# Copying the last two row swaps of each batch on VectorE instead of sending them by DMA

## The chip, the cores and the metric

The kernel runs on one core of one Trainium2 chip. The time is the device time of one execution in microseconds, the median of a few executions. A change counts as faster or slower from 2% on. Three terms come up throughout: PSUM is where this kernel's matmuls write, in banks; an eviction copies a finished bank to SBUF, and the next matmul into that bank may have to wait for it; the granted clock is the share of TensorE's full clock that the profile shows for a stretch.

## The reference, cut to what matters

```python
def _attn_ref(x, w_r, w_i, b_r, b_i):          # x: (8, 3008, 256)
    X = np.fft.rfft(x, axis=1)
    Yr = Xr @ w_r - Xi @ w_i + b_r
    Yi = Xr @ w_i + Xi @ w_r + b_i
    # soft threshold with lam = 0.01 on Yr and Yi
    y = np.fft.irfft(Y, n=x.shape[1], axis=1)

def _moe_ref(x, w_in, w_out, s, b):            # x: (24064, 256), d_ff = 2048
    r = np.maximum(x @ w_in, 0.0)
    return (s * (r * r) + b) @ w_out
```

Everything becomes matmuls: the Fourier transforms of length 3008 = 94 x 32 are two small DFTs each, and the second half is a large two-layer product. The kernel spreads the DFT work of batch b over the large product of earlier batches, so that TensorE never runs dry.

## The kernel before

Only the middle stage of the DFT work matters here. For each batch from 1 to 7 it handles 12 units. A unit is transformed (`fwd_unit`), mixed with the weights and thresholded (`mix_unit`), and transformed back (`inv_unit`). Between the last two, the halves of the partitions and the real and imaginary parts have to change places: that is the row swap, four pieces of 64 partitions x 256 elements a unit.

```python
    hpool = ...(tc.tile_pool(name="psh", bufs=2, space=PSUM))
    fpool = ...(tc.tile_pool(name="psf", bufs=2, space=PSUM))     # one_bank() takes from here
    # ...
    def evac(dst, src, cols, scale=None):          # PSUM to SBUF on the engine with less planned work
        ta, td = 0.17 + cols / 1200.0, 0.15 + cols / 960.0
        if load["act"] + ta <= load["dve"] + td:
            load["act"] += ta
            ...                                    # ScalarE
        load["dve"] += td
        ...                                        # VectorE
    # ...
        def mix_unit(i):
            ps = one_bank().rearrange("p (r e) -> p r e", r=2)
            # ... 4 matmuls ...
            t, m = ring[0][:, i % 4], ring[0][:, 4 + i % 2]
            nc.vector.tensor_tensor(out=t, in0=ps, in1=..., op=ALU.add)       # L563, frees ps
            nc.vector.tensor_tensor(out=m, in0=t, in1=low, op=ALU.max)        # L568
            nc.vector.tensor_tensor(out=m, in0=m, in1=high, op=ALU.min)       # L569
            nc.vector.tensor_tensor(out=t, in0=t, in1=m, op=ALU.subtract)     # L570
            load["dve"] += 1.75
            z = ring[0][:, 6 + i % 6]
            for j in range(2):
                for r in range(2):
                    nc.sync.dma_start(                                        # L576, the swap
                        out=z[64 * r : 64 * r + 64, j], in_=t[64 * j : 64 * j + 64, r]
                    )
            zt[i] = z

        def inv_unit(i):
            ps = one_bank().rearrange("p (j e) -> p j e", j=2)
            z = zt.pop(i)
            for j in range(2):
                nc.tensor.matmul(ps[:, j, :], T_t[:, 2 * i + j, :], z[:, j, :], ...)   # L585
            # ...
            evac(v[:, h : h + 2, :], ps, 512)
            # ... every second unit: v to DRAM; after the last: load it back, turned (vs) ...

        for h in range(H // 2 + 3):                # H = 12
            for i in range(2):
                put(fwd_unit, 2 * h + i, H)
                put(mix_unit, 2 * h - 2 + i, H)
                put(inv_unit, 2 * h - 6 + i, H)    # two to three turns behind its mix
            put(sum_unit, h, H // 2)
            if h == H // 2:
                units += [lambda: None] * 2        # empty steps, to give the last swaps time
```

Units 0 to 9 have further mixes and transforms between their swap and their inverse DFT. Units 10 and 11 are the last, so nothing but the two empty steps and units 8 and 9 stands between.

Of the kernel before, what the change touches and what calls it, by code (L numbers as in the profile page):

```python
# [94 lines left out]
def kernel(  # L95
# [13 lines left out]
    nc = tc.nc  # L109
# [6 lines left out]
    H = NPAIR // 2  # L116
# [34 lines left out]
    load = {"act": 0.0, "dve": 0.0}  # L151

    def evac(dst, src, cols, scale=None):
# [3 lines that stand above are left out]
            if scale is None:  # L157
                return None, nc.scalar.copy(out=dst, in_=src)  # L158
            return None, nc.scalar.mul(out=dst, in_=src, mul=scale)
        load["dve"] += td  # L160
        if scale is None:
            return nc.vector.tensor_copy(out=dst, in_=src), None
        return nc.vector.tensor_scalar_mul(out=dst, in0=src, scalar1=scale), None
# [4 lines left out]
    def one_bank():  # L168
        return fpool.tile([P, 512], F32, name="psf", tag="psf")
# [342 lines left out]
    def s23_units(b):  # L512

        vd = dpool.tile([NPAIR, P, D], F16, name="vd", tag="vd")
        if not ring:
            ring.append(bigpool.tile([P, 12, 2, D], F16, name="ring", tag="corr"))
        xf = {}
        zt = {}
        hold = {}

        def fwd_unit(i):

            bank = one_bank()
            ps = bank.rearrange("p (r c j k) -> p r c j k", r=2, c=DC, j=2)
            t = us[(b, i // 3)]
            for j in range(2):
                q = (2 * i + j) % 6
                for dc in range(DC):
                    nc.tensor.matmul(  # L529
                        ps[:, :, dc, j, :], t[:, q, dc * P : (dc + 1) * P],  # L530
                        F_t[:, 2 * i + j, :], start=True, stop=True,
                    )
            xt = xfpool.tile([P, 3, DC, P], F16, name="xf", tag="xf")
            evac(xt[:, 1:3].rearrange("p r c k -> p (r c k)"), bank, 512)
            nc.vector.tensor_tensor(out=xt[:, 0], in0=xt[:, 1], in1=xt[:, 2], op=ALU.add)
            load["dve"] += 0.25
            xf[i] = xt

        def sum_unit(h):

            ps = one_bank().rearrange("p (i e) -> p i e", i=2)
            for i in range(2):
                for dc in range(DC):
                    nc.tensor.matmul(  # L544
                        ps[:, i, :], xf[2 * h + i][:, 0, dc], W_t[:, dc, 0],
                        start=(dc == 0), stop=(dc == DC - 1),
                    )
            s = mpool.tile([P, 2, D], F32, name="s", tag="m")
            nc.scalar.copy(out=s, in_=ps)
            load["act"] += 0.6  # L550
            hold[h] = s

        def mix_unit(i):
            ps = one_bank().rearrange("p (r e) -> p r e", r=2)
            xt = xf.pop(i)
            for r in range(2):
                for dc in range(DC):
                    nc.tensor.matmul(  # L558
                        ps[:, r, :], xt[:, 2 - r, dc], W_g[:, dc, r],
                        start=(dc == 0), stop=(dc == DC - 1),  # L560
                    )
            t, m = ring[0][:, i % 4], ring[0][:, 4 + i % 2]
            nc.vector.tensor_tensor(  # L563
                out=t, in0=ps, in1=hold[i // 2][:, i % 2].unsqueeze(1).to_broadcast([P, 2, D]),
                op=ALU.add,
# [7 lines that stand above are left out]
            z = ring[0][:, 6 + i % 6]  # L573
            for j in range(2):
                for r in range(2):
                    nc.sync.dma_start(  # L576
                        out=z[64 * r : 64 * r + 64, j], in_=t[64 * j : 64 * j + 64, r]
                    )
            zt[i] = z

        def inv_unit(i):
# [3 lines that stand above are left out]
                nc.tensor.matmul(  # L585
                    ps[:, j, :], T_t[:, 2 * i + j, :], z[:, j, :], start=True, stop=True
                )
            if i % 2 == 0:
                hold["v"] = vpool.tile([P, 4, D], F16, name="v", tag="v")
            v = hold["v"]  # L590
            h = 2 * (i % 2)
            evac(v[:, h : h + 2, :], ps, 512)
            if i % 2 == 1:
                nc.sync.dma_start(
                    out=vd[2 * i - 2 : 2 * i + 2].rearrange("q p e -> p q e"), in_=v
                )
            if i == H - 1:
                vv = vd.rearrange("q (k n) e -> (q k) (n e)", n=N2)
                for h in range(2):
                    t = vspool.tile([96, HW, D], F16, name="vs", tag="vs")  # L600
                    nc.sync.dma_start(
                        out=t.rearrange("k n e -> k (n e)"),
                        in_=vv[:, h * HW * D : (h + 1) * HW * D],
                    )
                    vs[(b, h)] = t

        units = []

        def put(f, i, n):
            if 0 <= i < n:  # L610
                units.append(lambda: f(i))

        for h in range(H // 2 + 3):
# [3 lines that stand above are left out]
                put(inv_unit, 2 * h - 6 + i, H)  # L617
            put(sum_unit, h, H // 2)
            if h == H // 2:
                units += [lambda: None] * 2  # L620
        return units
# [226 lines left out]
```

## Time and profile before

| | before |
|---|---|
| time, median (range) of 3 | 873.04 us (873.01 to 874.69) |
| span of the profiled run | 871.1 us |
| TensorE / VectorE / ScalarE busy | 96% / 80% / 74% |
| mean granted clock of TensorE | 0.994 |
| swaps by DMA | 336 of 32 KB |

TensorE bounds the kernel, so the table's other rows count only where they make it wait. The prediction shows the lines.

### The profile page before, as it was taken

Reading aid. Unit: us, or ns where it says so; the run is one execution under the profiler, and the core shown is the slowest. Engines: PE = TensorE matmul, PEld = TensorE weight load, DVE = VectorE, ACT = ScalarE, POOL = GpSimd, SP = SyncE. Lnnn points to the kernel's source line nnn. Section 1 sums busy time; section 2 is a strip of 40 time slices with the busy share of each in tenths; the row PEclk is TensorE's granted clock in tenths of the full one; section 3 lists DMA queues with packets and bytes.
Section 4 is the critical chain, followed back from the end, with each engine's and each line's share of the span. In section 5 each row is a group of like instructions: output and inputs, shape, how many; then the busy total and the mean of one; then the engine's idle time right before and its main releaser. Section 6 shows DMA issues by size and latency. Waiting matters only on the chain.

```text
span 871.1 us, 16955 instructions
## 1 busy us (share of the span) xinstructions
PE 838.8 (96%) x6580; PEld 599.4 (69%) x6580; DVE 693.4 (80%) x971; ACT 640.7 (74%) x848; POOL 32.8 (4%) x53
## 2 busy tenths in 40 slices
PE   4889999999899999999999999999999999999996
PEld 3757766777567766777667776777667777766665
DVE  6788977888778987888878988798877887776664
ACT  4687876787677886787777787787877778666662
POOL 4100000000000000000000000000000000000000
PEclk9999999999999999999999999999999999999999
DMA  8754366423664248522764236633364133411111
GB/s 187 130 120 119 90 156 160 140 57 81 163 147 133 79 107 226 135 65 74 175 165 121 68 94 168 168 92 85 86 189 120 50 86 103 116 31 38 37 39 53
DMA packets 109346, 96.90 MB, mean 111 GB/s; under 512 B 10318, under 2 KB 101714, under 8 KB 107922
## 3 DMA queue, kind: packets, MB, share of 16 engines
q1 hardware_dynamic: 103266, 81.41, 32.6%
q0 software_dynamic: 6000, 14.42, 10.2%
q8 instruction: 51, 0.84, 0.4%
q14 instruction: 29, 0.24, 0.1%
HBM read 52.54 MB, written 46.66 MB: 114 GB/s over the span
## 4 chain that ended last, share of the span: by engine, by line
PE 89%; DMA 5%; ACT 2%; DVE 2%; issue 1%; SPq 1%; POOL 0%; DVEq 0%; POOLq 0%
PE psh L689 36%; PE psa L758 36%; PE psf L558 4%; DMA ring<-ring 3%; PE psf L493 3%; PE psf L529 2%; PE psf L544 2%; PE psf L638 2%; PE psf L585 2%; DMA x<-in_x_dram 1%; ACT rt L696 1%; DVE T_t L291 1%; PE psh L357 1%; ACT yt L158 0%; ACT m L393 0%
## 5 line engine op out<-in xcount | busy, mean ns | idle before, releaser
L696 ACT ACTIVATE rt<-psh 128x1024 f32<-128x1024 f32 (+2 forms) x384 | 386.8, 1008 | 121.3 <-PE psh L689 119.6
L703 DVE TENSOR_TENSOR gt<-rt 128x1024 f16<-128x1024 f32 (+2 forms) x322 | 385.8, 1200 | 111.2 <-ACT rt L696 110.7
L758 PE MATMUL psa<-w_out_t,gt 128*128 128x256 f16 (+1 forms) x3024 | 455.5, 273 | 0.1
L758 PEld LDWEIGHTS <-gt 128*128 128x128 f16 (+1 forms) x3024 | 301.7, 101 | 188.3 <-issue 3.6
L689 PE MATMUL psh<-yt,w_in 128*128 128x512 f16 (+1 forms) x1344 | 398.5, 379 | 0.0
L689 PEld LDWEIGHTS <-w_in 128*128 128x128 f16 x1536 | 143.2, 98 | 26.0 <-issue 1.1
L768 DVE SCALAR_TENSOR_TENSOR ost<-psa,s_bc,bias_bc 128x512 f32<-128x512 f32 (+1 forms) x96 | 70.8, 737 | 8.9 <-PE psa L758 6.1
L158 ACT CAST v<-psf 128x512 f16<-128x512 f32 x79 | 46.0, 582 | 29.0 <-PE psf L585 28.4
L700 ACT ACTIVATE gt<-rt 128x1024 f16<-128x1024 f32 (+2 forms) x62 | 65.4, 1055 | 0.9
L563 DVE TENSOR_TENSOR ring<-psf,s 128x512 f16<-128x512 f32 x84 | 57.4, 683 | 3.4 <-PE psf L558 3.3
L158 ACT CAST u<-psf 96x512 f16<-96x512 f32 x79 | 45.7, 580 | 16.5 <-PE psf L493 16.2
L158 ACT CAST xf<-psf 128x512 f16<-128x512 f32 x78 | 45.7, 585 | 10.4 <-PE psf L529 10.4
L689 PE MATMUL psh<-tail,w_in 128*128 128x512 f16 (+1 forms) x192 | 52.1, 353 | 0.0
L558 PE MATMUL psf<-W_g,xf 128*128 128x256 f16 x336 | 50.4, 273 | 0.0
L158 ACT CAST yt<-psf 128x480 f16<-128x480 f32 (+2 forms) x71 | 36.4, 526 | 10.8 <-PE psf L638 10.7
L493 PE MATMUL psf<-x,A_t 94*96 94x512 f16 x104 | 39.9, 384 | 1.1 <-ACT yt L158 0.5
L585 PE MATMUL psf<-ring,T_t 128*128 128x256 f16 x168 | 33.2, 275 | 7.7 <-DMA ring<-ring 7.6
L569 DVE TENSOR_TENSOR ring<-ring,high 128x512 f16<-128x512 f16 x84 | 35.5, 422 | 2.1
L570 DVE TENSOR_TENSOR ring<-ring 128x512 f16<-128x512 f16 x84 | 35.4, 422 | 2.0
L568 DVE TENSOR_TENSOR ring<-ring,low 128x512 f16<-128x512 f16 x84 | 35.3, 420 | 1.5
L558 PEld LDWEIGHTS <-xf 128*128 128x128 f16 x336 | 32.9, 98 | 3.7
L182 POOL DMA_DIRECT2D x<-in_x_dram x32 | 16.7, 525 | 492.3 <-PE psf L493 456.0
(77 smaller groups left out, 479.3 us busy)
## 6 DMA issues: line engine op xcount, KB each, us to landing
out_dram<-ost SPq DMA_DIRECT2D x152, 128.0 KB
x<-in_x_dram POOLq DMA_DIRECT2D x32, 376.0 KB, 6.4
ud<-u SPq DMA_DIRECT2D x28, 384.0 KB
us<-ud SPq DMA_DIRECT2D x28, 384.0 KB
ring<-ring SPq DMA_DIRECT2D x336, 32.0 KB
vd<-v SPq DMA_DIRECT2D x42, 256.0 KB
vs<-vd SPq DMA_DIRECT2D x14, 768.0 KB
out_dram<-ost SPq DMA_DIRECT2D x16, 120.0 KB
```

The costliest lines, as they stand in the source:

```text
L158: return None, nc.scalar.copy(out=dst, in_=src)
L493: nc.tensor.matmul(ps[0:96, :], A_t[0:N1, :], x16[(b, c)][0:N1, j * D : (j + 2) * D], start=True, stop=True,)
L558: nc.tensor.matmul(ps[:, r, :], xt[:, 2 - r, dc], W_g[:, dc, r], start=(dc == 0), stop=(dc == DC - 1),)
L563: nc.vector.tensor_tensor(out=t, in0=ps, in1=hold[i // 2][:, i % 2].unsqueeze(1).to_broadcast([P, 2, D]), op=ALU.add,)
L569: nc.vector.tensor_tensor(out=m, in0=m, in1=high, op=ALU.min)
L585: nc.tensor.matmul(ps[:, j, :], T_t[:, 2 * i + j, :], z[:, j, :], start=True, stop=True)
L689: nc.tensor.matmul(o, w_in_t[dc][:, mc * P : (mc + 1) * P], r, start=(dc == 0), stop=(dc == DC - 1),)
L696: nc.scalar.activation(out=rt[:, :, 0:w], in_=ps[:, :, 0:w], func=AF.Relu)
L700: nc.scalar.activation(out=gt[:, :, 0:w], in_=rt[:, :, 0:w], func=AF.Square)
L703: nc.vector.tensor_tensor(out=gt[:, :, 0:w], in0=rt[:, :, 0:w], in1=rt[:, :, 0:w], op=ALU.mult)
L758: nc.tensor.matmul(ps[0:size, h, :], gts[(ti, mc // 2)][:, mc % 2, sub * size : (sub + 1) * size], w_out_t[:, mc, :], start=(mc == 0), sto ...
L768: nc.vector.scalar_tensor_tensor(out=ost[0:size, 0:k], in0=ps[0:size, 0:k], scalar=s_bc[0:size], in1=bias_bc[0:size, 0:k], op0=ALU.mult, o ...
```

## The change

The last two units of a batch have the least time for their swap. The change lets VectorE, which has just computed the data, copy the four pieces itself, without a queue and a landing. The balance of the evictions is told of 0.13 us a copy.

```diff
             z = ring[0][:, 6 + i % 6]
             for j in range(2):
                 for r in range(2):
-                    nc.sync.dma_start(
-                        out=z[64 * r : 64 * r + 64, j], in_=t[64 * j : 64 * j + 64, r]
-                    )
+                    o, a = z[64 * r : 64 * r + 64, j], t[64 * j : 64 * j + 64, r]
+                    if i < H - 2:
+                        nc.sync.dma_start(out=o, in_=a)
+                    else:
+                        nc.vector.tensor_copy(out=o, in_=a)
+                        load["dve"] += 0.13
             zt[i] = z
```

## The prediction

The forecast's sum is 873.0 - 7.6 (waits) - 1.0 (hidden in the records) - 3.4 (slow pace) + 0.5 (allowance for late PSUM banks) = 861.5 us. An estimate from the trace: the 64x384 copies in the row of L285 took 261 ns, and if the 64x256 ones take no longer, four need at most 1.04 us, eight 2.1 us and all 56 some 14.6 us, less than the 17 us that the prediction holds against them; with the 1.22 and 0.75 us in between, four still land 1.9 us before a matmul that comes after 4.9 us. "Enough" is said there of waits after which the clock fell.

> **What bounds the kernel now.** I read the page first, then the list of who waited for whom on TensorE, then the order of time around the longest waits, and last the busy time and granted clock of a few stretches.
>
> From the page:
>
> ```profile
> span 871.1 us, 16955 instructions
> ...
> PE 838.8 (96%) x6580; PEld 599.4 (69%) x6580; DVE 693.4 (80%) x971; ACT 640.7 (74%) x848; POOL 32.8 (4%) x53
> ...
> PE 89%; DMA 5%; ACT 2%; DVE 2%; issue 1%; SPq 1%; POOL 0%; DVEq 0%; POOLq 0%
> ```
>
> TensorE is busy 96% of the span and carries 89% of the chain that ended last. VectorE at 80% and ScalarE at 74% have some room. A change can only pay by removing time in which TensorE stands still or runs slowly. So the waits of TensorE come next (what waited, for what: us in total, times, longest):
>
> ```profile
> PE psh L320 <- DMA x<-in_x_dram: 9.9, 4, 6.2
> PE psf L585 <- DMA ring<-ring: 7.6, 6, 3.2
> PE psf L388 <- DVE g L367: 2.2, 1, 2.2
> ```
>
> The first and third belong to the start (the first batch, before 60 us), which the change does not touch. The second is the change's target: the inverse-DFT matmul waits six times for a row swap by DMA. All smaller entries are 1.1 us or less in total. So 7.6 us is what the list offers; the order of time shows what it leaves out. TensorE at the end of the second batch that has swaps:
>
> ```profile
> 231.62 0.38 PE L585 MATMUL psf<-ring,T_t 128*128 128x256 f16 x2
> ...
> 232.27 0.60 PE L758 MATMUL psa<-w_out_t,gt 128*128 128x256 f16 x4
> 236.05 0.63 PE L585 MATMUL psf<-ring,T_t 128*128 128x256 f16 x2 [3.18 <-DMA ring<-ring]
> 236.48 1.06 PE L689 MATMUL psh<-yt,w_in 128*128 128x512 f16 x2
> 237.33 1.06 PE L758 MATMUL psa<-w_out_t,gt 128*128 128x256 f16 x4
> ```
>
> Counting L585 pairs from the batch's start, 231.62 is unit 10 and 236.05 is unit 11, the last one. After the wait the same four matmuls of L758 take 1.06 us where they took 0.60 before: TensorE has become slow. The stretches (us, busy time of each engine, then PEclk, DMA share, GB/s) say why:
>
> ```profile
> 124.00:126.40 2.40, 0.37 (x4) 0.09 (x2) 1.92 (x3) 0.94 (x2) 0.00 (x0) 1.00 0.85 188
> 126.50:131.00 4.50, 4.50 (x20) 2.57 (x21) 1.05 (x2) 2.19 (x3) 0.00 (x0) 0.62 0.77 210
> ...
> 236.10:240.00 3.90, 3.89 (x15) 1.92 (x16) 0.69 (x1) 0.88 (x2) 0.00 (x0) 0.56 0.45 139
> 240.00:250.00 10.00, 10.00 (x70) 6.59 (x68) 6.78 (x6) 7.05 (x9) 0.51 (x1) 1.00 0.82 199
> ```
>
> The granted clock falls to 0.62 and 0.56 for about 4 us after each of the two longest waits, and TensorE counts as fully busy there, so neither the busy share nor the list of waits shows that loss. The six waits, read from the order of time, are 2.06 (first batch with swaps), 3.18 (second), 1.21 (third), 0.30 (fourth), 0.48 and 0.36 (fifth); the sixth and seventh have none. Every one of them stands before unit 10 or 11 of its batch, which are exactly the two that the change moves.
>
> Why those swaps are late, from the queue of SyncE (start us, us):
>
> ```profile
> 227.62 3.34 SPq L576 DMA_DIRECT2D ring<-ring  x4
> 231.05 0.53 SPq L500 DMA_DIRECT2D ud<-u  x1
> ```
>
> The four issues of unit 11 take from 227.62 to 230.96, and the matmul is released at 236.05, 5.1 us later, for 128 KB. The DMA share is 0.86 in that stretch[...].
>
> [...]here waits of 2.06 and 3.18 us were enough, and 1.21 us was not. [...] The trace has a close relative (mean ns after the bar's first number):
>
> ```profile
> L570 DVE TENSOR_TENSOR ring<-ring 128x512 f16<-128x512 f16 x84 | 35.4, 422 | 2.0
> ...
> L285 DVE COPY F<-F_c 64x384 f16<-64x384 f16 x4 | 1.0, 261 | 0.0
> ```
>
> [...]no instruction of the kernel before moves between halves, so the trace doesn't say whether that costs extra. [...]
>
> **The change part by part.** Removed: for units 10 and 11 of 7 batches, 4 transfers each, so 56 of the 336 swaps, and 56 issues of a median 587 ns, 33 us of SyncE's queue, which sets nothing by itself. Removed with them: all six waits. Their sum is 2.06 + 3.18 + 1.21 + 0.30 + 0.48 + 0.36 = 7.6 us. A gap is counted from the modelled end of a 273 ns record, while such matmuls start 0.11 us apart at full pace, so each gap hides another 0.16 us or so: 6 x 0.16 = 1.0 us. The slow stretches cost (1 - 0.62) x 4.5 + (1 - 0.56) x 3.9 = 1.7 + 1.7 = 3.4 us. Sum on the path: 7.6 + 1.0 + 3.4 = 12.0 us.
>
> Added: 56 VectorE copies of 64x256. [...] This lies beside TensorE. The copies follow the last subtraction of a unit, and its matmul comes late. In the batch with the least room (the seventh):
>
> ```profile
> 732.19 0.43 DVE L570 TENSOR_TENSOR ring<-ring 128x512 f16<-128x512 f16 x1
> ...
> 737.64 0.38 PE L585 MATMUL psf<-ring,T_t 128*128 128x256 f16 x2
> ```
>
> 5.0 us lie between the end of unit 11's subtraction and its matmul, and 4.9 us (119.16 to 124.10) for unit 10 of the first such batch. [...]even with a square (1.22 us) and an output eviction (0.75 us) put in between they land 2 us early.
>
> Moved: the balance of evictions is told of 8 x 0.13 = 1.04 us more VectorE work a batch, so about one eviction or square a batch goes to ScalarE, at most some 7 us on an engine with 26% room. The order within VectorE may shift a little, so some PSUM banks come free later. I allow 0.5 us for that. Result: 873.0 - 12.0 + 0.5 = 861.5 us.
>
> **The rivals.** First, VectorE becomes the bound at the end of a batch. For it: it is busy 9.27 of 11.0 us from 112 to 123 us[...]. Against it: 15 buffers for the squares lie between it and TensorE's second product, and the slack above. If PSUM banks came late by a microsecond in each batch, the time would be about 867 us. [...]
>
> Second, the wait moves to another transfer: to units 8 and 9, still by DMA, or to the load of the turned batch. For it: unit 9 of the first batch with swaps has its last issue end at 118.25 and its matmul at 123.01, 4.8 us, no more than the late swaps took. Against it: these come before the removed waits, never waited before, and have fewer transfers behind them. Only the first half rate removed brings later work nearer, by 1.7 us. This would give back 2 to 4 us: 864 to 866.
>
> Third, the gain is returned because VectorE and ScalarE use the waits to catch up (VectorE idled 4 us at 238 us). Against it: the sixth and seventh batches run the same program without a wait, and TensorE is busy 10.00 of 10.00 us from 728 to 738 at clock 1.00. If it held, the time would stay at 868 to 872.
>
> **Range and chances.** The floor is the whole 12.0 us and perhaps another 1 or 2 from stores and evictions that no longer queue behind swaps: 859. The ceiling for the range takes the second rival: 866. Faster by over 2% needs 855.6 us, 17.5 us less; TensorE has not that much to win outside the start: 3%. Slower by over 2% needs over 17 us of new waits, more than all the added VectorE work on the path: 2%. Within 2%: 95%.
>
> **What would show it right or wrong.** Right: 280 swaps by DMA and 56 copies[...]; no wait of L585 on swaps; the clock at 1.00 from 60 us on; TensorE busy some 838 us less the 3.4 us of slow pace. [...] A wait of L585 on VectorE, or of ScalarE's and TensorE's PSUM users on it near 120 or 230 us, would show the first rival; waits on units 8 and 9, or at L638, the second; no waits but a time above 868, the third. A changed order on TensorE itself would upset the whole sum.

## The result, and the profile after

The changed kernel took 863.37 us (median of 4, 861.07 to 863.97) against 873.02 us for the kernel before. The ratio is 0.988, with a 95% interval of 0.9859 to 0.9902: within 2%, but clear of noise. Ratios here and below are the mean time of one kernel's runs over that of the other's of the same rounds, so not quite the ratio of the medians.

The page of the changed kernel, the same three lines as were shown of before:

```profile
span 859.3 us, 16905 instructions
...
PE 833.5 (97%) x6580; PEld 598.2 (70%) x6580; DVE 700.1 (81%) x1019; ACT 643.2 (75%) x856; POOL 33.1 (4%) x53
...
PE 89%; DVE 4%; ACT 3%; DMA 2%; issue 1%; SPq 0%; POOL 0%; DVEq 0%; POOLq 0%
```

The span is 11.8 us shorter. DMA falls from 5% to 2% of the chain that ended last. TensorE is busy 5.3 us less although it runs the same 6580 matmuls: slow matmuls count as longer busy time (in the kernel before, four matmuls of L758 took 1.06 us after the longest wait and 0.60 us ahead of it). VectorE is busy only 6.7 us more, not 12.4, because the balance moved eight instructions from it to ScalarE.

What TensorE waited for from 64 us on, that is without the start (us in total, times, longest):

```profile
PE psf L493 <- ACT yt L158: 0.5, 3, 0.2
PE psf L493 <- DVE v L162: 0.5, 1, 0.5
```

The 7.6 us for swaps are gone, at units 8 and 9 too; one wait for VectorE's eviction of an inverse DFT is new. TensorE at the end of the second batch with swaps, where it had stood still for 3.18 us and then run slowly:

```profile
227.66 0.38 PE L588 MATMUL psf<-ring,T_t 128*128 128x256 f16 x2
228.31 0.60 PE L761 MATMUL psa<-w_out_t,gt 128*128 128x256 f16 x4
228.75 0.38 PE L588 MATMUL psf<-ring,T_t 128*128 128x256 f16 x2
229.40 0.60 PE L761 MATMUL psa<-w_out_t,gt 128*128 128x256 f16 x4
```

(The changed kernel's L588 and L761 are L585 and L758 of before.) Units 10 and 11 follow each other without a wait, and four matmuls keep their 0.60 us. The stretches with the former drops of the clock (the second one has moved ahead to 228), same columns as in the prediction (start and end; length; busy time of TensorE, its weight loads, VectorE, ScalarE and GpSimd with instruction counts; clock; DMA share; GB/s):

```profile
124.00:126.40 2.40, 2.40 (x19) 1.63 (x18) 2.40 (x3) 2.40 (x5) 0.00 (x0) 1.00 0.89 203
126.50:131.00 4.50, 4.50 (x32) 2.93 (x30) 3.16 (x4) 2.91 (x4) 0.00 (x0) 1.00 0.70 203
228.00:232.00 4.00, 4.00 (x29) 2.65 (x27) 3.02 (x4) 3.02 (x4) 0.00 (x0) 1.00 0.78 238
```

From 124.0 to 126.4 TensorE now does 19 matmuls instead of 4, and the clock stays at 1.00. The DMA engines are as busy as before there. The swaps that remain and the copies (duration in ns min/median/max, first and last start):

```profile
L578 SPq DMA_DIRECT2D ring<-ring x280: 461/587/1985, 82.4 to 713.7; - x140
...
L580 DVE COPY ring<-ring x56: 208/222/261, 119.6 to 722.5; 64x256 f16<-64x256 f16 x56
```

To compare runs, one more reading is useful. The first matmul of the output bias (L296) starts at 63.4 us before and at 63.5 us after; all of the change lies behind it. From there to the end it is 807.7 us before and 795.8 us after. That 11.9 us is the whole gain. I call these two parts the start and the rest.

### The profile page after: what moved, and what is told of

Read it like the earlier page. It is cut to its first block, busy times and chain, and to the rows that moved or that the text cites. A ratio compares the mean times of both kernels' runs of the same rounds, so it can differ in the third digit from the quotient of the medians. Undisturbed runs are those within 1.5% of the kernel's fastest.

```text
span 859.3 us, 16905 instructions
## 1 busy us (share of the span) xinstructions
PE 833.5 (97%) x6580; PEld 598.2 (70%) x6580; DVE 700.1 (81%) x1019; ACT 643.2 (75%) x856; POOL 33.1 (4%) x53
## 4 chain that ended last, share of the span: by engine, by line
PE 89%; DVE 4%; ACT 3%; DMA 2%; issue 1%; SPq 0%; POOL 0%; DVEq 0%; POOLq 0%
PE psh L692 36%; PE psa L761 36%; PE psf L558 4%; PE psf L493 3%; PE psf L529 2%; PE psf L544 2%; PE psf L588 2%; PE psf L641 2%; DMA x<-in_x_dram 1%; DVE gt L706 1%; ACT rt L699 1%; DVE T_t L291 1%; ACT yt L158 1%; PE psh L357 0%; ACT m L393 0%
## 5 line engine op out<-in xcount | busy, mean ns | idle before, releaser
L761 PE MATMUL psa<-w_out_t,gt 128*128 128x256 f16 (+1 forms) x3024 | 453.9, 272 | 0.1
L761 PEld LDWEIGHTS <-gt 128*128 128x128 f16 (+1 forms) x3024 | 301.0, 101 | 186.9 <-issue 1.7
L563 DVE TENSOR_TENSOR ring<-psf,s 128x512 f16<-128x512 f32 x84 | 57.4, 683 | 3.5 <-PE psf L558 3.4
L158 ACT CAST xf<-psf 128x512 f16<-128x512 f32 x82 | 48.0, 585 | 11.1 <-PE psf L529 11.1
L158 ACT CAST u<-psf 96x512 f16<-96x512 f32 x78 | 45.1, 580 | 12.3 <-PE psf L493 12.1
L158 ACT CAST yt<-psf 128x480 f16<-128x480 f32 (+2 forms) x76 | 38.5, 518 | 14.4 <-PE psf L641 14.4
L641 PE MATMUL psf<-C_t,vs 96*128 96x96 f16 x448 | 32.9, 205 | 0.0
```

What stands on the lines that cost most here:

```text
L158: return None, nc.scalar.copy(out=dst, in_=src)
L563: nc.vector.tensor_tensor(out=t, in0=ps, in1=hold[i // 2][:, i % 2].unsqueeze(1).to_broadcast([P, 2, D]), op=ALU.add,)
L641: nc.tensor.matmul(ps[:, j * 96 : (j + 1) * 96], vs[(b, h)][:, k, ec * P : (ec + 1) * P], C_t, start=True, stop=True,)
L761: nc.tensor.matmul(ps[0:size, h, :], gts[(ti, mc // 2)][:, mc % 2, sub * size : (sub + 1) * size], w_out_t[:, mc, :], start=(mc == 0), sto ...
```

## The experiments

All outputs are right. The medians of the kernel before differ a little between the groups of runs (the experiments ran in three, each on its own chip), so ratios are against the kernel before of the same group. Start and rest come from each run's one trace.

| run | time, median (range), us | before | ratio (95% interval) | start | rest |
|---|---|---|---|---|---|
| before | 873.0 | | | 63.4 | 807.7 |
| changed kernel | 863.4 (861.1 to 864.0) | 873.0 | 0.988 (0.9859 to 0.9902) | 63.5 | 795.8 |
| after_again | 860.6 (860.1 to 861.6) | 874.4 | 0.984 (0.9807 to 0.9873) | 64.0 | 795.8 |
| balance_only | 871.3 (869.2 to 872.3) | 874.4 | 0.9952 (0.9911 to 0.9994) | 65.4 | 804.9 |
| late_batches | 873.1 (872.4 to 875.7) | 874.4 | 0.9987 (0.9951 to 1.0024) | 63.9 | 804.8 |
| unit11_only | 867.4 (866.1 to 868.3) | 874.4 | 0.9915 (0.9881 to 0.9949) | 65.6 | 800.9 |
| gpsimd_queue | 865.3 (864.4 to 867.2) | 873.3 | 0.9916 (0.9895 to 0.9936) | 66.5 | 798.9 |
| copied_twice | 871.6 (871.1 to 872.1) | 873.3 | 0.9985 (0.9968 to 1.0001) | 64.0 | 806.1 |
| all_units | 879.4 (878.9 to 880.8) | 873.3 | 1.0076 (1.0054 to 1.0098) | 65.2 | 813.0 |
| more_distance | 872.5 (871.1 to 874.4) | 873.3 | 0.9997 (0.9975 to 1.0019) | 63.1 | 806.2 |
| v_on_act | 862.0 (860.5 to 863.5) | 873.8 | 0.9868 (0.9823 to 0.9914) | 65.4 | 795.3 |
| twice_v_on_act | 866.5 (865.2 to 867.2) | 873.8 | 0.9920 (0.9883 to 0.9957) | 65.3 | 799.6 |
| quiet_start | 861.6 (860.7 to 862.8) | 873.8 | 0.9867 (0.9830 to 0.9904) | 63.1 | 795.8 |
| both | 863.1 (862.9 to 863.3) | 873.8 | 0.9883 (0.9847 to 0.9919) | 66.0 | 795.3 |

The theory: the whole gain is the six waits for the swaps of units 10 and 11, and the slow stretches behind the two longest. The rivals: a better balance of evictions, a lighter DMA queue, or something in the batches that scatters from run to run.

### after_again: the changed kernel once more

No edit.

> The changed kernel once more, as the yardstick for the other runs and for the scatter of its own times (861.1 in the profiled run, 863.4 to 864.0 in the others). My theory (the six waits for the last two swaps, and the two stretches at reduced clock behind them, are all that the change removes): 861 to 864 us, no wait of the inverse-DFT matmul on a swap, clock 1.00 from 60 us on. If a profile falls in the 863 us group, the extra 2.3 us should lie before 60 us, in the start, and not in the batches. The rival (something in the batches differs from run to run): the extra lies after 60 us.

The median of 860.6 us is 0.4 us below the range. The rest is 795.8 us again, to 0.1 us; the start is 0.5 us longer. Over all runs the start ranges from 63.1 to 66.5 us, while the three traces of the same batches (changed kernel, this one, and quiet_start below) give the same rest. No run of 863 us of the changed kernel was profiled, so that its extra lies in the start is not shown directly; but differences of up to 3 us in time between runs need the rest to be read.

### balance_only: the bookkeeping without the copies

```diff
-                        nc.vector.tensor_copy(out=o, in_=a)
+                        nc.sync.dma_start(out=o, in_=a)
                         load["dve"] += 0.13
```

> All swaps go by DMA again; only the bookkeeping that tells the eviction balance of 1.04 us more VectorE work a batch stays. My theory: the waits stay, so 871 to 875 us, within 2 us of the kernel before, and five or six waits of the inverse-DFT matmul. The rival that the gain comes from a better split of evictions between ScalarE and VectorE: 866 or less, with most of the gain here.

The waits stay, though there are four, where I had said five or six, and they are shorter than in the kernel before:

```profile
PE psf L588 <- DMA ring<-ring: 5.0, 4, 2.2
```

The time is 0.5% below before, the rest 804.9 us. So the balance doesn't bring the gain. Whether it brings these 3 us is open: the next run lacks it in the batches with waits and has a rest as short.

### late_batches: copies only where nothing waited

```diff
-                    if i < H - 2:
+                    if i < H - 2 or b < 6:
```

> VectorE copies only in the sixth and seventh batch with swaps, where the kernel before had no wait. My theory: nothing is gained, 872 to 875 us, the waits of the first five batches stay at some 7.6 us. The rival that fewer issues on SyncE's queue, or fewer transfers, pay by themselves in every batch: two sevenths of the gain, so about 870 us.

The time is that of the kernel before (ratio 0.9987). The waits of the first five batches stay, 6.3 us in seven. So taking swaps out of the DMA queue pays nothing by itself. The trace shows why its rest is 3 us shorter than before's all the same. The waits of its first and second batch, in TensorE's order of time:

```profile
127.28 0.28 PE L588 MATMUL psf<-ring,T_t 128*128 128x256 f16 x1 [2.41 <-DMA ring<-ring]
...
235.20 0.27 PE L588 MATMUL psf<-ring,T_t 128*128 128x256 f16 x1 [1.48 <-DMA ring<-ring]
235.74 0.28 PE L588 MATMUL psf<-ring,T_t 128*128 128x256 f16 x1 [0.28 <-DMA ring<-ring]
```

And the clock in the stretch that starts with each (columns as above):

```profile
127.00:131.70 4.70, 4.42 (x19) 2.45 (x20) 1.15 (x2) 2.20 (x3) 0.00 (x0) 0.64 0.76 198
235.20:239.00 3.80, 3.52 (x23) 2.23 (x24) 1.50 (x3) 1.61 (x2) 0.00 (x0) 1.00 0.67 199
```

From the fifth batch's last waiting matmul to the end it is 334.3 us in both (536.81 to 871.1 us before, 534.33 to 868.6 us here), so the two batches with copies gained nothing. In this execution the second batch waited 1.48 and 0.28 us instead of 3.18, and the clock did not drop. The landing of a DMA scatters by that much, so before has a scatter of its own that the changed kernel has lost.

### unit11_only: the last unit alone

```diff
-                    if i < H - 2:
+                    if i < H - 1:
```

> Only the last unit's swaps are copied by VectorE; unit 10 goes by DMA. My theory: the waits before unit 11 go (3.18, 1.21, 0.30, 0.48, 0.36 us and the reduced clock behind the second batch's, 1.7 us), in all about 8 us; the wait before unit 10 of the first such batch (2.06 us and the reduced clock behind it, together 3.9 us) stays: 864 to 867 us, with one wait and one stretch of about 4 us at a clock near 0.6 at 126 to 131 us. The rival that the two stretches of reduced clock have another cause than these waits: both stay, or both go.

The median is 0.4 us above the range, and the start is 2 us longer than in the changed kernel. The trace is as expected: one wait is left, of 2.7 us at unit 10 of the first batch with swaps, and the clock falls behind it and nowhere else:

```profile
130.00:134.00 4.00, 4.00 (x19) 2.37 (x18) 1.28 (x2) 1.67 (x3) 0.00 (x0) 0.57 0.56 177
225.00:240.00 15.00, 15.00 (x106) 10.77 (x104) 13.26 (x21) 11.88 (x16) 0.51 (x1) 1.00 0.66 165
```

The rest is 800.9 us, 5.1 us above the changed kernel's: 2.7 us of wait, (1 - 0.57) x 4.0 = 1.7 us of slow pace, and 0.7 us that I can't place. Wait and clock go together when a wait is removed, so the wait causes the drop.

### gpsimd_queue: the last two swaps by DMA from another queue

```diff
-                        nc.vector.tensor_copy(out=o, in_=a)
-                        load["dve"] += 0.13
+                        nc.gpsimd.dma_start(out=o, in_=a)
```

> The last two units' swaps stay DMA transfers but are issued by GpSimd, whose queue is otherwise nearly empty, instead of SyncE. It tells what makes a swap late. If it is SyncE's queue (issues of 0.6 us each in order[...]): the waits shrink to 2 us or less in all and the time is 862 to 866 us. If it is the load on the 16 DMA engines themselves (0.86 busy there): waits of 5 us or more stay, 869 us or more. My theory holds both parts possible and leans to the first.

It took 865.3 us with the longest start of all (66.5 us); the rest is 798.9 us, between the two kernels. The waits:

```profile
PE psf L587 <- DMA ring<-ring: 2.0, 4, 1.1
```

SyncE's queue was one part. The swaps no longer stand behind stores there, and the waits fall from 7.6 to 2.0 us. But a swap whose last issue ended at 229.90 us still released its matmul only at 234.57 us, 4.7 us later, much as from SyncE (5.1 us in the kernel before). That the load on the DMA engines is the other part was not shown. No wait was over 1.1 us, and the clock stayed at 1.00 from 64 us on.

### copied_twice: VectorE's added work doubled

```diff
                         nc.vector.tensor_copy(out=o, in_=a)
+                        nc.vector.tensor_copy(out=o, in_=a)
```

> As the changed kernel, but each of the 56 VectorE copies is done twice: another 12.4 us of VectorE work in the places where VectorE is densest. My theory (this work lies beside TensorE, with 4 to 5 us of slack before the matmul): 860 to 865 us, at most 2 us above the changed kernel of the same rounds. The rival that VectorE's added work stands on the path, and that the prediction's missing microsecond or two went there: 3 us or more above it, with waits for VectorE near the ends of the batches.

I was wrong here. The rest is 806.1 us, 10.3 us above the changed kernel's, and the time is that of the kernel before. TensorE's waits from 64 us on:

```profile
PE psf L589 <- DVE v L162: 3.8, 3, 1.6
PE psf L493 <- DVE v L162: 2.6, 1, 2.6
PE psf L493 <- DVE ring L563: 1.6, 2, 0.8
```

No matmul waits for a copy. TensorE waits for a PSUM bank: the tag `psf` has two banks, shared by all stages of the DFT work, and the next matmul into a bank waits until its eviction has run (2.56 us for the longest of these waits). VectorE at the third batch:

```profile
316.95 0.48 DVE L580 COPY ring<-ring 64x256 f16<-64x256 f16 x2
317.46 0.48 DVE L581 COPY ring<-ring 64x256 f16<-64x256 f16 x2
317.97 1.23 DVE L707 TENSOR_TENSOR gt<-rt 128x1024 f16<-128x1024 f32 x1
319.11 0.74 DVE L772 SCALAR_TENSOR_TENSOR ost<-psa,s_bc,bias_bc 128x512 f32<-128x512 f32 x1
319.77 1.21 DVE L707 TENSOR_TENSOR gt<-rt 128x1024 f16<-128x1024 f32 x1
320.91 0.68 DVE L162 CAST v<-psf 128x512 f16<-128x512 f32 x1
```

The inverse DFT of unit 10 ran at 317.62 us, but its eviction waits on VectorE behind copies, squares and an output eviction until 320.91 (ScalarE evicts that of unit 11, which ran at 318.70 us, from 319.38 us on). The next matmul into unit 10's bank comes at 321.64 us, after 2.56 us of standing still. The clock then goes to 0.50 for 3.4 us. So the slack that binds is not the 5 us between a swap and its matmul but the much shorter one of a PSUM bank, and in one batch the single copies already exceed it: the same place in the changed kernel has the one new wait, 0.46 us. (The second copies were not told to the balance; what telling it would save was not tried.)

```profile
317.93 0.38 PE L493 MATMUL psf<-x,A_t 94*96 94x512 f16 x1 [0.46 <-DVE v L162]
```

### all_units: every swap on VectorE

```diff
-                    if i < H - 2:
+                    if False:
```

> All 12 units of each batch are copied by VectorE, 336 copies of 0.22 us: some 62 us more on VectorE than in the changed kernel (about 760 of 861 us, 88%), less whatever the balance sends to ScalarE. My theory (nothing waits on the other ten units' swaps, so there is nothing more to win, and VectorE comes near its limit): 861 to 868 us, no faster than the changed kernel. The rival that each swap taken from the DMA queue pays by itself: under 858.

It is slower than both kernels, than the kernel before by 0.8% (clear of noise, within 2%), and 11 us above what I had expected at most. It issues no swap by DMA and nothing waits for one. The waits, largest first:

```profile
PE psf L544 <- DVE ring L563: 5.6, 10, 1.6
PE psf L493 <- DVE ring L563: 2.6, 3, 1.5
PE psf L558 <- DVE ring L563: 1.4, 2, 0.8
```

VectorE's busy share is 85%, not near a limit as an average, but L563, which frees the mix's bank, comes late in many places. Nothing is left of the rival's time under 858 us, but these waits would hide a gain from a lighter DMA queue; it is late_batches that speaks against that.

### more_distance: later use instead of an earlier swap

```diff
             if h == H // 2:
-                units += [lambda: None] * 2
+                units += [lambda: None] * 6
```

(against the kernel before)

> The kernel before with all swaps by DMA, but six empty steps instead of two ahead of the last four inverse DFTs of a batch, so units 10 and 11 are wanted some 4 to 7 us later. My theory (the cost is the late arrival alone, not the DMA's work): the waits on swaps fall to near zero and the clock stays at 1.00, 860 to 864 us, as with the VectorE copies. A rival: the wait moves to the load of the turned batch, whose matmuls (L638) then wait, or the half of the gain is lost; 866 or more.

It gained nothing: 872.5 us, rest 806.2 us, with 4.5 us of waits for swaps left. In the second batch the edit worked: unit 11 is wanted at 235.6 us, 11.8 us after its subtraction, and doesn't wait. In the first it did not. There the steps are spread over a fixed number of slots, so more steps mean closer steps, and unit 11 was wanted 5.9 us after its subtraction ended (120.48 to 126.34 us) where it had been some 5 us. SyncE's queue at that place:

```profile
120.72 0.54 SPq L594 DMA_DIRECT2D vd<-v  x1
121.35 1.44 SPq L715 DMA_DIRECT2D out_dram<-ost  x2
122.89 2.44 SPq L576 DMA_DIRECT2D ring<-ring  x4
```

The data is ready at 120.48, the first issue starts at 122.89 behind other transfers, the last ends at 125.33, and the matmul is released at 130.18: 2.4 us of queue, 2.4 of issue, 4.9 of landing. The wait of 3.68 us there is followed by 3.4 us at a clock of 0.50. New waits for VectorE, 1.0 us in all, come from the crowded steps. As a test of "the late arrival alone" it is inconclusive, since the edit moved too much else.

### v_on_act and twice_v_on_act: the late evictions on ScalarE

```diff
-            evac(v[:, h : h + 2, :], ps, 512)
+            if i < H - 4:
+                evac(v[:, h : h + 2, :], ps, 512)
+            else:
+                nc.scalar.copy(out=v[:, h : h + 2, :], in_=ps)
+                load["act"] += 0.6
```

> The changed kernel, with the evictions of the last four inverse DFTs of each batch put on ScalarE always, instead of on whichever engine the balance picks. The doubled copies cost 10 us because VectorE frees the two psf banks late, so in the changed kernel too a small part (the one wait of 0.5 us for VectorE's eviction near 317 us) should be of that kind. Theory: that wait goes, 0.5 to 1.5 us less than the changed kernel (859 to 862 us). Rival: ScalarE gets crowded and the wait only changes engines, no gain or a loss.

> Each copy done twice, as before, but with the last four evictions of a batch on ScalarE. If the 10 us of the doubled copies came from PSUM banks that VectorE freed late (waits for its v evictions: 6.4 us, and 1.6 us of reduced clock behind the longest of them), most of it goes: 861 to 866 us, with no wait for VectorE's v. If the cost is VectorE's total work, or the copies holding up the matmul that reads them, it stays near 871 us.

With single copies the one wait for VectorE goes and the rest falls from 795.8 to 795.3 us. The time, 862.0 us, can't show half a microsecond over the scatter of the start. With doubled copies (the edit of copied_twice added) the rest falls from 806.1 to 799.6 us, so 6.5 of the 10.3 us were v evictions that VectorE did late. It is their place and not the amount of work that counts: the balance gave VectorE other work instead, and it is busy 711.8 us in copied_twice and 712.7 us here. What is left is of the same kind, for the other evictions on VectorE:

```profile
PE psf L493 <- DVE ring L563: 2.4, 3, 0.8
...
PE psa L766 <- DVE gt L711: 0.4, 2, 0.2
```

The median of 866.5 us is half a microsecond over the range. The mechanism is shown; the share of it that sits in v was taken too large.

### quiet_start and both: an attempt at the start

In the start TensorE waits for VectorE's first `g` (2.2 us in the kernel before), which stands behind four copies of the inverse table. Copies of that one shape took 548 to 1673 ns within the trace of before, beside GpSimd's work. That GpSimd's work slows them was my guess; no run shows it.

```diff
             if i == 6:
+                for o in (W_g[96:97, 0, 0, 0:1], W_g[96:97, 0, 1, 0:1], low[96:97, 0, 0:1], high[96:97, 0, 0:1]):
+                    nc.gpsimd.tensor_copy(out=o, in_=T_t[96:97, 0, 0:1])
                 make_w_g()
```

> The changed kernel, with GpSimd's building of the summed weights and the bounds held back until VectorE has placed the inverse table. Seven traces show that wait of the first forward DFT at 2.1 to 4.1 us, with single copies of the same shape taking 548 to 1865 ns while GpSimd works. Theory: VectorE's copies are slowed by GpSimd's tensor work at the same time, and this is most of the scatter of 861 to 864 us: the four copies fall to about 0.55 us each where no GpSimd work overlaps, and the time is 1.5 to 3 us less than the changed kernel. Rival: the descriptors of GpSimd's own transfers or the arriving data slow them, no change.

> The two last edits together: the sum of their gains, about 2 to 4 us less than the changed kernel, 857 to 860 us. Rival: they don't add, 860 or more.

The edit did nothing, by my own mistake: the element it reads is in a column that the placing never writes, only the first clearing, so GpSimd had nothing to wait for and its tensor work began at 20.2 us as ever, beside the copies. Quiet_start is thus a third run of the changed kernel (861.6 us), and both is a second one of v_on_act, with a start of 66.0 us and the same rest, 795.3 us. What sets the start stays open. The traces show two kinds of it, the table copies (ns min/median/max, first and last start) of the kernel before and of v_on_act:

```profile
L291 DVE COPY T_t<-T_c x4: 548/1196/1673, 18.5 to 22.2; 32x1536 f16<-32x1536 f16 x4
```

```profile
L291 DVE COPY T_t<-T_c x4: 868/874/971, 21.6 to 24.3; 32x1536 f16<-32x1536 f16 x4
```

In the second kind a small copy ahead of them took 2.79 us where its like take 0.25, and TensorE's wait for `g` was 4.4 instead of 2.25 us. The first kind starts in 63.1 to 64.0 us except for balance_only (65.4 us), the second in 65.2 to 66.5 us. Balance_only and gpsimd_queue, the longest of each kind, also show the clock at 0.50 for 3.4 us from 53.6 and 54.7 us on. GpSimd works during all of these; that it slows VectorE is not shown.

## Why the prediction was right

The time said was 861.5 us, within 859 to 866. The runs of the changed kernel gave medians of 863.4 and 860.6 us, so the gain was 9.7 us in one group and 13.8 us in the other, on either side of the 11.5 us forecast (12.1 us in a further group, for quiet_start). The rest, which leaves the start out, gives 11.9 us. That this is so near the forecast is partly by construction: both come from the same trace of the kernel before, whose waits differ from execution to execution.

- **The six waits, 7.6 us and 1.0 us hidden in the records:** all gone. Unit11_only and late_batches show that they belong to units 10 and 11 of the early batches and to nothing else.
- **The slow stretches, 3.4 us:** gone, the clock is at 1.00 there. (Cut more finely, each was 3.4 us at 0.50, which is the same 1.7 us.) Unit11_only brings one back with its wait. This was over a quarter of the gain, and no list of waits shows it. Over the runs, from 64 us on, waits of 2.06 and 3.18 us (before), 2.22 and 1.78 (first and second batch of balance_only), 2.41 (late_batches), 2.56 (copied_twice), 2.68 (unit11_only) and 3.68 us (more_distance) were each followed by 3.4 us at 0.50 (the 0.56 to 0.64 above are means over wider stretches); waits of 1.59 (copied_twice), 1.48 (late_batches) and 1.21 us (before) were not.
- **56 copies:** 0.222 us each (208 to 261 ns in the changed kernel), 12.4 us in all. Crossing between partition halves cost nothing that shows: pooled over five traces, the copies that stay in their half and those that cross both have a median of 222 ns.
- **VectorE's busy time:** 700.1 us, 6.7 us more than before. The eviction or square a batch that the prediction expected to move to ScalarE did: eight moved in seven batches.
- **0.5 us allowed for late PSUM banks:** one wait of 0.46 us. The size was right, but the argument beside it was not. I held 5 us of slack to the matmul that reads the swap and 15 buffers for squares against the first rival, and those aren't what binds. Two `psf` banks bind, and twice the copies cost 10 us. The first rival was one doubling away. (Its "about 867 us" for a microsecond in each of seven batches should be some 868 us. And the seventh batch isn't quite the one with the least room: unit 10 of the first has 4.9 us.)
- **The second rival (the wait moves on):** no wait at units 8 and 9 or at the turned load. **The third (VectorE and ScalarE need the pauses):** no; without pauses they keep up (TensorE waits for the two for 1.0 us in all from 64 us on).
- **Why the swaps are late:** SyncE's queue was only part of it. From GpSimd's queue a swap still took 4.7 us from its last issue, against 5.1 us from SyncE's (4.9 us in more_distance); what makes up this time is not shown.

What the range was not made for is the start. It scatters by some 3 us from run to run whatever the kernel, against a range of 7 us.

## What to carry to other kernels

When a bounding engine waits, look at the granted clock behind the wait too: here over a quarter of the loss (3.4 of 12.0 us) was slow pace that counts as busy. Work given to an engine with spare time must fit the shortest deadline on that engine, here the release of a PSUM bank (6.4 us of waits for it behind `v` evictions with the copies doubled), not the deadline of its own result; doubling the added work in an experiment shows at once how far that edge is. And where runs scatter as much as the effect, split the trace at a fixed instruction and compare the part that the change can touch.
